# FNet mixing and a SwiGLU block on one core: the first chunk's preparation in another order, the split gate at another unit, the transforms one unit earlier

## The chip, the cores and the metric

The kernel runs on one core of one Trainium2 chip. The metric is the device time of one execution in microseconds (us). A core has five engines that run side by side, each through its own list of instructions in order: PE multiplies matrices (PEld is its loading of weights), DVE does elementwise work, ACT does elementwise work with functions (sine, SiLU, copies), POOL does elementwise work without access to PSUM and issues some transfers, and SP issues most transfers (DMA). They wait for each other by semaphores. Matmul results are written to PSUM, which has eight banks of 128 x 512 float32; all other tiles lie in SBUF.

## The reference

```python
def _attn_ref(x):                    # x: 8 x 3008 x 256
    X = np.fft.fft(x, axis=1)
    X = np.fft.fft(X, axis=2)
    return X.real.astype(np.float32)

def _moe_ref(x, w_gate, w_val, w_out):        # 24064 x 256, Dff = 1536
    g = x @ w_gate
    silu = g * (1.0 / (1.0 + np.exp(-g)))
    val = x @ w_val
    return (silu * val @ w_out).astype(np.float32)
```

The output of the first is the input of the second. The result is 24064 x 256 in float32.

## The kernel before, in words

**The mathematics.** The Fourier transform along the sequence (length M = 3008 per batch, 8 batches) is folded by symmetry: rows r and M - r, and the quarters of the sequence, are added and subtracted, so that a product with a quarter of the table (`Tab`, made on the chip from sines and cosines) is enough. The transform along the 256 features is not carried out on the data; it is multiplied into the weights. So there are two half inputs, an even one `Pt` and an odd one `Qt`, and two transformed weights, `Wp` (cosine) and `Wq` (sine); a row is Pt Wp + Qt Wq, and its mirror image in the sequence is Pt Wp - Qt Wq. `Wm` is -2 Wq (its row 0 zeroed by `m2`), so that adding Qt Wm to a finished accumulator turns a row's result into that of its mirror image. Each weight has a gate half (index 0) and a value half (index 1).

**The folds.** A batch's rows are treated as chunk A (128 rows of each quarter) and chunk C (60 more, and row 0 of the sequence). For batch 0 the rows are loaded to `XA` and `XC0`, and PE, DVE and ACT take part in the preparation: PE brings rows to their places by a product with a permutation (`place`, L417 to L425), DVE adds the mirrored rows (`sums`, L427 to L432), ACT writes the halves in bfloat16 (`halves`, `minus`, L434 to L439), and PE multiplies these unfolded halves with the table (`unfolded`, L448 to L464; eo = 0 makes Pt, eo = 1 makes Qt; ch = 0 is chunk A, ch = 1 chunk C). For the other batches POOL does the folding (`fold_steps`, L186 to L217) and PE the product (`transform`, L607 to L668). POOL also folds batch 0, for the second part of its frequencies (L552 to L567).

**The order of the preparation of batch 0** is written out by hand (L504 to L571 and L672 to L679), and each engine executes its instructions in just this order of the program: place and sums of A, halves of A, the second table, `d_tables`, unfolding of A for eo 0 and eo 1, weighting of the table (`weigh`), loads of the second weight third, POOL's steps on the table (L524 to L530), loads of the third; place, sums, halves of C; the transforms of the first third of the weights (`transform_w`, L467 to L483, for gate and value, each with CD and SDt); folds of A and of C on POOL, with the load of `Wo` between; loads of the next batch on SP; then unfolding of C, `transform` of batch 0's first part, which on DVE writes Pt and Qt, and `value_rows` (L485 to L502), products of one column that give the weights' share of row 0 in `w0`.

`transform_w` has two halves: two matmuls, and copies to SBUF that run when the returned function is called. The copies are one for `Wp` (k = 0, on DVE or ACT, L482), and for `Wq` (k = 1) one on ACT (L476) and then one multiply on POOL that makes `Wm` (L480; on ACT for the second third, L478). The first third's `Wm` is read from the first unit on.

**The main loop** (L1045 to L1081) runs over units (t, f): 24 tiles t of up to 512 columns, 12 blocks f of 128 of Dff. The tiles are 480, 512, 512 wide, the same again, 17 of 512, and a last one of 320. `part_a` multiplies gate g and value v with Pt and Qt; ACT forms SiLU(g) (`sg`) and DVE the product `hp` (L882, L898). In the next unit `part_b` adds the Wm product (L907), which gives the mirrored g (and v, in units that aren't split), and the mirrored product `hm` is formed by POOL (L912) or DVE (L916). Units that are `split` get the mirrored value without PE: DVE keeps the even part in `es` (L874) and takes 2 es - v (L885, L888). Tile 0 is all whole units. In `seeded` units (f in SEED = 1, 3, 10) ACT puts row 0's share into the accumulator (L809) and copies es (L872), which saves DVE its step L874. Between these products, PE does `OWork`: the product of the previous tile's hp and hm with `Wo` (L770), eight matmuls a unit, evicted by ACT (L730) and stored by SP (L736).

**The split gate.** In units with f in GATED and t >= 4, if split, the mirrored gate too comes from DVE: `gate_even` (L814) starts the gate product one unit early and DVE keeps its even part `eg` (L823), `gate_odd` (L827) adds the Qt product, and `mirrored` (L835) forms 2 eg - g. This saves PE one matmul of the tile's width, and costs DVE two steps. GATED is (2,): the gate's share of row 0 is an extra column of `w0`, made in `value_rows` of the weight third to which f belongs (thirds of four blocks).

**The transforms in the loop.** Batch b has two parts, (b, 0) and (b, 1). `slot` (L919) says at which unit the transform of a part is emitted: 4 units into the tile before the one that needs it; its second half (eo = 1) comes one unit later for part 0 and two units later for part 1. `seq` (L921 to L936) spreads POOL's folds ahead of these slots. Part (0, 1) is at unit 9 in both kernels.

`psG` and `psV` are lines of three PSUM banks each, used in turn; `psO` has two.

Of the kernel before, what the change touches and what calls it, by code (L numbers as in the profile page):

```python
# [31 lines left out]
def kernel(  # L32
# [8 lines left out]
    nc = tc.nc  # L41
# [61 lines left out]
    Tab = const.tile([P, 2, 2, 2, NTAB], BF16, name="Tab")  # L103
    halfpi = const.tile([P, 1], F32, name="halfpi")
    zero = const.tile([P, 1], F32, name="zero")
    GATED = (2,)
    w0 = const.tile([P, nF + len(GATED)], F32, name="w0")
    sel = const.tile([P, P], BF16, name="sel")
    CD = const.tile([P, 2, P], BF16, name="CD")
# [253 lines left out]
    def weigh(lo, hi):  # L363
        vts(Tab[:, 1, 1, :, lo:hi], Tab[:, 1, 1, :, lo:hi], scalar1=wC, scalar2=None, op0=Alu.mult)
# [73 lines left out]
    def minus(SB, S, a=0):  # L438
        nc.scalar.activation(SB[:, 2, a:a + 2], S[:, a:a + 2, :, P:D], AF.Copy, scale=-1.0)  # L439
# [27 lines left out]
    def transform_w(fc, gv, k, ps):  # L467
        dst, tab = ((Wp, CD), (Wq, SDt))[k]
        src = W0[gv] if fc == 0 else Wraw[gv][:, :, (fc - 1) * T:fc * T]
        fs = slice(fc * T, (fc + 1) * T)  # L470
        for no in range(2):
            nc.tensor.matmul(ps, tab[:, no, :], src[:, no, :], start=(no == 0), stop=(no == 1))

        def copies():
            if k:
                nc.scalar.copy(dst[:, gv, fs], ps)  # L476
                if fc == 1:
                    nc.scalar.activation(Wm[:, gv, fs], ps, AF.Copy, scale=m2)  # L478
                else:
                    pts(Wm[:, gv, fs], dst[:, gv, fs], scalar1=m2, scalar2=1.0, op0=Alu.mult, op1=Alu.mult)  # L480
            else:
                (nc.scalar.copy if gv and fc else nc.vector.tensor_copy)(dst[:, gv, fs], ps)  # L482
        return copies  # L483

    def value_rows(fcs):  # L485

        n = T // P
        ps = psO.tile([P, T], F32, name="o")
        for fc in fcs:
            src = W0[1] if fc == 0 else Wraw[1][:, :, (fc - 1) * T:fc * T]  # L490
            for f in range(n):
                for no in range(2):
                    nc.tensor.matmul(ps[:, fc * n + f:fc * n + f + 1], src[:, no, f * P:(f + 1) * P],
                                     SDt[:, no, 0:1], start=(no == 0), stop=(no == 1))
        nc.scalar.copy(w0[:, fcs[0] * n:(fcs[-1] + 1) * n], ps[:, fcs[0] * n:(fcs[-1] + 1) * n])
        for k, f in enumerate(GATED):
            if f // n in fcs:
                src = W0[0] if f < n else Wraw[0][:, :, (f // n - 1) * T:f // n * T]
                for no in range(2):
                    nc.tensor.matmul(ps[:, nF + k:nF + k + 1], src[:, no, f % n * P:(f % n + 1) * P],  # L500
                                     SDt[:, no, 0:1], start=(no == 0), stop=(no == 1))
                nc.scalar.copy(w0[:, nF + k:nF + k + 1], ps[:, nF + k:nF + k + 1])  # L502

    psA = place(XA, putA, 4, ((psG, "g"), (psV, "v")))  # L504
    sums(SA, XA, psA)
# [11 lines left out]
    d_tables()  # L517
    nc.vector.memset(SDt[:, :, 0:1], 1.0)
    unfolded(0, 0, SBa, True, False)
    unfolded(1, 0, SBa, True, False)  # L520
    weigh(0, NCE)

    load_w(1)
    nc.gpsimd.iota(kfO, pattern=[[4, G]], base=1, **iota)  # L524
# [4 lines left out]
    ptt(hd, SA[:, 0:2, :, 0:1], SA[:, 2:4, :, 0:1], op=Alu.add)  # L529
    heads(nc.gpsimd, hd[:, 0], hd[:, 1], CEa)  # L530
    load_w(2)
    psC = place(XC0, putC, 2, ((psO, "o"),))
    sums(SC, XC0, psC)
    halves(SBc, SC)
    minus(SBc, SC)
    wts = []
    for gv in range(2):
        for k, (pool, nm) in enumerate((((psV, "v"), (psG, "g")), ((psO, "o"), (psO, "o")))[gv]):
            wts.append(transform_w(0, gv, k, pool.tile([P, T], F32, name=nm)))
    heads(nc.vector, SC[:, 0, :, 0:1], SC[:, 1, :, 0:1], CEc)  # L540
    raO = SD.rearrange("p k a d -> p (k a d)")[:, 0:4 * G].rearrange("p (c q n) -> p c q n", c=2, q=2)

# [133 lines left out]
            row0(CE, slice(0, P), q, ch, q, acc[1][q])  # L676
    unfolded(1, 1, SBc, False, True)
    transform(0, 0, (1,), acc)
    value_rows((0,))  # L679

    tmp_ctx.close()
# [156 lines left out]
    def part_a(u):  # L838
        t, f = u
        n = width(t)  # L840
        w = n + (B if t == nT - 1 else 0)
        fs = slice(f * P, (f + 1) * P)
        if f == 0:
            hts[t] = (hp.tile([P, nF, T + B], BF16, name="hp"), hp.tile([P, nF, T], BF16, name="hm"))
        Pt, Qt = pq_tiles(t)

        def mm(ps, Wt, gv, src, start, stop):
            nc.tensor.matmul(ps[:, :w], Wt[:, gv, fs], src[:, :w], start=start, stop=stop,  # L848
                             skip_group_check=True)

        if gated(u):
            g, sg, _ = gates[u]
        else:
            g = psG.tile([P, T], F32, name="g")
            mm(g, Wp, 0, Pt, True, False)
            if u == (0, 0):
                v = psV.tile([P, T], F32, name="v")
                mm(v, Wp, 1, Pt, True, False)
            mm(g, Wq, 0, Qt, False, True)
        if split(u):  # L860
            mine = u in seeded
            e = seeded.pop(u) if mine else psV.tile()
            mm(e, Wp, 1, Pt, not mine, False)
            if not mine:
                psV.begun[id(e)] = w
            if not gated(u):
                sg = sgp.tile([P, T], F32, name="sg")
                nc.scalar.activation(sg[:, :w], g[:, :w], AF.Silu)  # L868
            stt = nc.vector.scalar_tensor_tensor
            es = next_es()  # L870
            if mine:
                nc.scalar.copy(es[:, :n], e[:, :n])  # L872
            else:
                stt(es[:, :n], bc[t][:, :n], w0[:, f:f + 1], e[:, :n], op0=Alu.mult, op1=Alu.add)  # L874

            def odd():
                if mine:
                    nc.tensor.matmul(e[:, :w], Wz[:, SEED.index(f), :], Qt[:, :w], start=False, stop=True,  # L878
                                     skip_group_check=True)
                else:  # L880
                    mm(e, Wq, 1, Qt, False, True)
                nc.vector.tensor_tensor(hts[t][0][:, f, :w], sg[:, :w], e[:, :w], op=Alu.mult)  # L882
# [12 lines left out]
        mm(v, Wq, 1, Qt, False, True)  # L895
        sg = sgp.tile([P, T], F32, name="sg")
        nc.scalar.activation(sg[:, :w], g[:, :w], AF.Silu)  # L897
        nc.vector.tensor_tensor(hts[t][0][:, f, :w], sg[:, :w], v[:, :w], op=Alu.mult)  # L898
        state[u] = (g, v)
# [221 lines left out]
```

## Time and profile before

| | |
|---|---|
| time, median of 3 runs | 625.33 us (625.13 to 625.45) |
| the profiled execution | 625.21 us |
| its span, first to last instruction | 623.3 us |
| busy: PE / DVE / POOL / ACT | 98% / 92% / 85% / 76% of the span |
| moved by DMA | 55.42 MB, mean 89 GB/s |
| unit (0,0) begins on PE | 23.66 us |

The profile gives busy time and share of each engine, and the trace lists every instruction with start and duration on the span's clock. In rows of a timeline, the first number is the start and the second the duration of a group of equal instructions that follow each other (x4 is four of them); in brackets stands how long the engine was idle before it, and what ended the wait. L and a number is the line of the kernel. Matmuls are pipelined: a row's duration holds the latency of the last, and a stream of them is read from start to start. In a table of windows, each row is a stretch from A to B with its length and then each engine's busy time in it. The rows that matter stand in the prediction.

### The profile page before, as it was taken

The page shows a single profiled execution, that of the slowest core. Times are in us where ns is not written, and L with a number is a line of the kernel's source. Part 1 is how long each engine was busy: PE and PEld are TensorE (multiplying, and loading weights), DVE is VectorE, ACT ScalarE, POOL GpSimd, SP SyncE. Part 2 cuts the span into 40 slices and gives each one's busy share as a digit, 9 for nine tenths or more (in the row PEclk, how much of TensorE's full clock was granted, in tenths as well). Part 3 has the DMA queues.
Part 4 walks back from the last instruction along what each step waited for, and adds up shares of the span by engine and source line. Part 5 has one row for each costly group of instructions (what it writes and reads, how often), then busy time and mean ns, then how long its engine had stood idle before and what let it go on. Part 6 is the DMA issues. An engine that isn't in the chain of part 4 may idle for free.

```text
span 623.3 us, 13287 instructions
## 1 busy us (share of the span) xinstructions
PE 610.8 (98%) x4124; PEld 396.4 (64%) x4190; DVE 575.3 (92%) x1053; ACT 470.8 (76%) x880; POOL 527.2 (85%) x543
## 2 busy tenths in 40 slices
PE   9999999999999999999999999999999999999997
PEld 6446666666666666666666666666666666666686
DVE  7889999999999999999999999999999999999991
ACT  7687868778777787787777877877787778778773
POOL 9997989899899989997997989998799856656661
PEclk9999999999999999999999999999999999999999
DMA  8682442244222253244245111134121111111112
GB/s 226 122 171 77 114 139 84 84 115 138 81 67 86 70 151 108 74 134 127 70 109 149 50 44 55 48 85 139 58 59 37 53 45 42 59 52 44 58 52 77
DMA packets 52981, 55.42 MB, mean 89 GB/s; under 512 B 7504, under 2 KB 44238, under 8 KB 52910
## 3 DMA queue, kind: packets, MB, share of 16 engines
q1 hardware_dynamic: 49726, 52.20, 29.2%
q0 software_dynamic: 3184, 2.36, 2.6%
q8 instruction: 33, 0.54, 0.4%
q14 instruction: 38, 0.31, 0.2%
HBM read 32.22 MB, written 24.67 MB: 91 GB/s over the span
## 4 chain that ended last, share of the span: by engine, by line
PE 87%; DVE 6%; ACT 3%; issue 2%; DMA 1%; SPq 0%; POOL 0%; DVEq 0%; ACTq 0%
PE o L770 37%; PE v L848 18%; PE g L848 15%; PE g L907 8%; PE v L620 2%; PE v L878 2%; DVE hp L882 2%; DVE VV L888 1%; DMA XA<-in_x_dram 1%; PE g L620 1%; ACT EV L730 1%; PE g L819 1%; ACT sg L868 1%; PE g L832 1%; DVE hm L916 1%
## 5 line engine op out<-in xcount | busy, mean ns | idle before, releaser
L912 POOL TENSOR_TENSOR hm<-sgv,VV 128x512 bf16<-128x512 f32 (+2 forms) x258 | 322.7, 1258 | 76.7 <-DVE VV L888 66.2
L911 ACT ACTIVATE sgv<-g 128x512 f32<-128x512 f32 (+2 forms) x258 | 153.7, 596 | 62.3 <-PE g L907 55.9
L882 DVE TENSOR_TENSOR hp<-sg,v 128x512 bf16<-128x512 f32 (+2 forms) x273 | 184.1, 675 | 7.6 <-PE v L848 6.2
L868 ACT ACTIVATE sg<-g 128x512 f32<-128x512 f32 (+2 forms) x253 | 151.5, 599 | 30.9 <-PE g L848 20.9
L770 PE MATMUL o<-Wo,hp 128*128 128x256 bf16 (+2 forms) x1140 | 169.6, 273 | 0.1
L770 PE MATMUL o<-Wo,hm 128*128 128x256 bf16 (+2 forms) x1140 | 169.7, 273 | 0.0
L770 PEld LDWEIGHTS <-hm 128*128 128x128 bf16 (+2 forms) x1140 | 112.0, 98 | 70.4 <-issue 2.5
L770 PEld LDWEIGHTS <-hp 128*128 128x128 bf16 (+2 forms) x1140 | 112.0, 98 | 67.8 <-issue 3.4
L888 DVE SCALAR_TENSOR_TENSOR VV<-SDf,v 128x512 f32<-128x512 f32 (+2 forms) x179 | 120.5, 673 | 0.0
L848 PE MATMUL v<-Pt,Wp 128*128 128x512 bf16 (+2 forms) x288 | 107.9, 375 | 5.2 <-DVE hm L916 0.8
L848 PE MATMUL g<-Pt,Wp 128*128 128x512 bf16 (+2 forms) x268 | 100.7, 376 | 0.1
L907 PE MATMUL g<-Qt,Wm 128*128 128x512 bf16 (+2 forms) x267 | 100.0, 375 | 0.7 <-ACT sg L897 0.7
L874 DVE SCALAR_TENSOR_TENSOR SDf<-bc,w,v 128x512 f32<-128x512 bf16 (+2 forms) x116 | 85.1, 734 | 0.2
L848 PE MATMUL v<-Qt,Wq 128*128 128x512 bf16 (+2 forms) x222 | 83.1, 374 | 0.0
L848 PEld LDWEIGHTS <-Wp 128*128 128x128 bf16 x556 | 54.2, 98 | 41.3 <-issue 7.1
L848 PE MATMUL g<-Qt,Wq 128*128 128x512 bf16 (+2 forms) x205 | 76.5, 373 | 0.0
L874 DVE SCALAR_TENSOR_TENSOR es<-bc,w,v 128x512 f32<-128x512 bf16 (+2 forms) x91 | 66.9, 735 | 0.1
L809 ACT ACTIVATE v<-bc,w 128x512 f32<-128x512 bf16 (+2 forms) x66 | 45.2, 685 | 24.1 <-DVE VV L888 23.7
L730 ACT COPY EV<-o 128x512 f32<-128x512 f32 x90 | 52.8, 586 | 4.8 <-PE o L770 4.8
L888 DVE SCALAR_TENSOR_TENSOR VV<-es,v 128x512 f32<-128x512 f32 (+2 forms) x79 | 53.2, 673 | 0.0
L848 PEld LDWEIGHTS <-Wq 128*128 128x128 bf16 x490 | 47.9, 98 | 8.0 <-issue 0.5
L872 ACT COPY SDf<-v 128x512 f32<-128x512 f32 (+2 forms) x66 | 39.1, 592 | 0.0
(189 smaller groups left out, 642.5 us busy)
## 6 DMA issues: line engine op xcount, KB each, us to landing
out_dram<-EV SPq DMA_DIRECT2D x96, 128.0 KB
XA<-in_x_dram SPq DMA_DIRECT2D x32, 256.0 KB
XA<-in_x_dram SPq DMA_DIRECT2D x112, 64.0 KB
XC<-in_x_dram SPq DMA_DIRECT2D x210, 16.0 KB
XC<-in_x_dram SPq DMA_DIRECT2D x56, 60.0 KB
bc<-row SPq DMA_DIRECT2D x20, 128.0 KB
out_dram<-EV SPq DMA_DIRECT2D x12, 120.0 KB
out_dram<-EV SPq DMA_DIRECT2D x10, 112.0 KB
```

Of the source, the lines that this page charges most:

```text
L730: nc.scalar.copy(ev[:, 0:len(pair), :], ps[:, 0:len(pair), :])
L770: nc.tensor.matmul(ps[:n, j, :], hts[minus][:, f, c:c + n], Wo[:, f, :], start=(f == 0), stop=(f == nF - 1))
L809: nc.scalar.activation(e[:, :w], bc[t][:, :w], AF.Copy, scale=w0[:, f:f + 1])
L848: nc.tensor.matmul(ps[:, :w], Wt[:, gv, fs], src[:, :w], start=start, stop=stop, skip_group_check=True)
L868: nc.scalar.activation(sg[:, :w], g[:, :w], AF.Silu)
L872: nc.scalar.copy(es[:, :n], e[:, :n])
L874: stt(es[:, :n], bc[t][:, :n], w0[:, f:f + 1], e[:, :n], op0=Alu.mult, op1=Alu.add)
L882: nc.vector.tensor_tensor(hts[t][0][:, f, :w], sg[:, :w], e[:, :w], op=Alu.mult)
L888: stt(vm[:, n - 1::-1], es[:, :n], 2.0, e[:, :n], op0=Alu.mult, op1=Alu.subtract)
L907: nc.tensor.matmul(ps[:, :w], Wm[:, gv, f * P:(f + 1) * P], Qt[:, :w], start=False, stop=True, skip_group_check=True)
L911: nc.scalar.activation(sg[:, w - 1::-1], g[:, :w], AF.Silu)
L912: nc.gpsimd.tensor_tensor(hts[t][1][:, f, :w], sg[:, :w], v[:, :w], op=Alu.mult)
```

## The change

It does three things, in one diff.

1. In the preparation of batch 0, `place` and `sums` of chunk C stand between the two unfoldings of A, and `halves` and `minus` of C behind the weighting of the table. The transforms of the value half of the first weight third move behind the unfolding and transform of C, to stand ahead of `value_rows`; the gate half stays where it was. The copy of a value half's `Wp` is always on ACT. In unit (0,0) the four products come in the order g, g, v, v instead of g, v, g, v.
2. The split gate is at f = 11 instead of 2. Its column of `w0` so comes from the last third of the weights; `value_rows` issues its products ahead of the first copy. In the last tile f = 11 is a whole unit, so there the gate is not split.
3. `slot` is 3 units into the tile instead of 4: transforms are emitted at units 3 and 4 (part 0) or 3 and 5 (part 1).

```diff
-    GATED = (2,)
+    GATED = (11,)
...
-                (nc.scalar.copy if gv and fc else nc.vector.tensor_copy)(dst[:, gv, fs], ps)
+                (nc.scalar.copy if gv else nc.vector.tensor_copy)(dst[:, gv, fs], ps)
...
+        more = [(k, f) for k, f in enumerate(GATED) if f // n in fcs]
+        for k, f in more:
+            src = W0[0] if f < n else Wraw[0][:, :, (f // n - 1) * T:f // n * T]
+            for no in range(2):
+                nc.tensor.matmul(ps[:, nF + k:nF + k + 1], src[:, no, f % n * P:(f % n + 1) * P],
+                                 SDt[:, no, 0:1], start=(no == 0), stop=(no == 1))
         nc.scalar.copy(w0[:, fcs[0] * n:(fcs[-1] + 1) * n], ps[:, fcs[0] * n:(fcs[-1] + 1) * n])
-        for k, f in enumerate(GATED):
...
+        for k, f in more:
+            nc.scalar.copy(w0[:, nF + k:nF + k + 1], ps[:, nF + k:nF + k + 1])
...
     unfolded(0, 0, SBa, True, False)
+    psC = place(XC0, putC, 2, ((psO, "o"),))
+    sums(SC, XC0, psC)
     unfolded(1, 0, SBa, True, False)
     weigh(0, NCE)
+    halves(SBc, SC)
+    minus(SBc, SC)
...
     load_w(2)
-    psC = place(XC0, putC, 2, ((psO, "o"),))
-    sums(SC, XC0, psC)
-    halves(SBc, SC)
-    minus(SBc, SC)
-    wts = []
-    for gv in range(2):
-        for k, (pool, nm) in enumerate((((psV, "v"), (psG, "g")), ((psO, "o"), (psO, "o")))[gv]):
-            wts.append(transform_w(0, gv, k, pool.tile([P, T], F32, name=nm)))
+    wts = [transform_w(0, 0, k, pool.tile()) for k, pool in enumerate((psV, psG))]
...
     transform(0, 0, (1,), acc)
+    for fn in [transform_w(0, 1, k, psO.tile([P, T], F32, name="o")) for k in range(2)]:
+        fn()
     value_rows((0,))
...
-            if u == (0, 0):
-                v = psV.tile([P, T], F32, name="v")
-                mm(v, Wp, 1, Pt, True, False)
...
-        if u != (0, 0):
-            v = psV.tile([P, T], F32, name="v")
-            mm(v, Wp, 1, Pt, True, False)
+        v = psV.tile([P, T], F32, name="v")
+        mm(v, Wp, 1, Pt, True, False)
...
-    slot = {(b, part): max(first_tile[(b, part)] - 1, 0) * nF + 4 for b, part in jobs}
+    slot = {(b, part): max(first_tile[(b, part)] - 1, 0) * nF + 3 for b, part in jobs}
```

More of the change, by code (lines that the diff above doesn't have):

```diff
@@ L494, in value_rows @@
                                      SDt[:, no, 0:1], start=(no == 0), stop=(no == 1))
-        nc.scalar.copy(w0[:, fcs[0] * n:(fcs[-1] + 1) * n], ps[:, fcs[0] * n:(fcs[-1] + 1) * n])
-        for k, f in enumerate(GATED):
[L497 to L502, printed above, removed]
+        more = [(k, f) for k, f in enumerate(GATED) if f // n in fcs]
[4 more added lines that the diff above has]
+                                 SDt[:, no, 0:1], start=(no == 0), stop=(no == 1))
+        nc.scalar.copy(w0[:, fcs[0] * n:(fcs[-1] + 1) * n], ps[:, fcs[0] * n:(fcs[-1] + 1) * n])
+        for k, f in more:
+            nc.scalar.copy(w0[:, nF + k:nF + k + 1], ps[:, nF + k:nF + k + 1])
     psA = place(XA, putA, 4, ((psG, "g"), (psV, "v")))
```

## The prediction

> **What bounds the kernel now.** I read the table of engines first, then busy times by stage, then each engine's timeline up to 40 us.
>
> ```profile
> PE 610.8 (98%) x4124; PEld 396.4 (64%) x4190; DVE 575.3 (92%) x1053; ACT 470.8 (76%) x880; POOL 527.2 (85%) x543
> ```
> ```profile
> 26.40:48.80 22.40, 20.43 (x109) 9.53 (x110) 17.86 (x33) 19.40 (x41) 20.72 (x33) 1.00 0.71 149
> 48.80:600.00 551.20, 545.95 (x3691) 355.21 (x3753) 525.50 (x931) 423.81 (x792) 475.99 (x451) 1.00 0.29 82
> ```
>
> The first row gives PE 98% of the span. The other two are stages: length, then busy time of PE, PEld, DVE, ACT and POOL. From 48.8 us on PE lacks 551.20 - 545.95 = 5.25 us in 551. It has almost nothing to gain there and no slack in which lost time could be made up. In tile 0 (26.4 to 48.8) it lacks 22.40 - 20.43 = 1.97 us. So this kernel is PE's instruction stream in order, and every microsecond for which PE stands still early on is added to the end. What matters is when PE can do each step of the prologue. PE's timeline (start, duration, line):
>
> ```profile
> 13.52 0.81 PE L463 MATMUL v<-Tab,SBa 128*128 128x377 bf16 x4
> ...
> 16.09 1.88 PE L422 MATMUL o<-XC,putC 128*128 128x512 f32 x4
> 17.81 0.38 PE L472 MATMUL v<-W,CD 128*128 128x512 bf16 x1
> ...
> 18.83 0.60 PE L472 MATMUL o<-W,CD 128*128 128x512 bf16 x2
> ...
> 19.70 0.89 PE L463 MATMUL v<-Tab,SBc 128*128 128x377 bf16 x4
> ...
> 23.02 0.34 PE L493 MATMUL o<-SDt,W 128*128 128x1 bf16 x8
> ...
> 23.66 0.36 PE L848 MATMUL g<-Pt,Wp 128*128 128x480 bf16 x1
> ...
> 26.20 0.37 PE L907 MATMUL g<-Qt,Wm 128*128 128x480 bf16 x1
> 26.41 0.37 PE L907 MATMUL v<-Qt,Wm 128*128 128x480 bf16 x1
> ```
>
> It is a nearly unbroken chain: the second unfolding of A begins at 13.52, chunk C is placed at 16.09, gate weights follow at 17.81, value weights at 18.83, the unfolding of C at 19.70, and unit (0,0) at 23.66. The row at 26.41 is the one on which the forecast hangs: the mirrored value product of unit (0,0), which reads Wm's value half. The multiply L480 on POOL makes Wm:
>
> ```profile
> 17.52 0.82 POOL L367 TENSOR_SCALAR Tab<-Tab 128x752 bf16<-128x752 bf16 x1
> ...
> 18.87 0.79 POOL L373 DMA_DIRECT2D EV<-in_moe_w_gate_dram  x1
> 19.66 0.73 POOL L373 DMA_DIRECT2D EV<-in_moe_w_val_dram  x1
> 20.99 1.36 POOL L480 TENSOR_SCALAR Wm<-Wq,m 128x512 bf16<-128x512 bf16 x2 [0.60 <-ACT Wq L476]
> 22.31 1.08 POOL L198 TENSOR_TENSOR EOf<-SA 128x512 f32<-128x512 f32 x1
> ...
> 37.61 1.36 POOL L480 TENSOR_SCALAR Wm<-Wq,m 128x512 bf16<-128x512 bf16 x2
> ```
>
> Both halves, gate and value, are multiplied at 20.99 (x2, 0.68 us each), and only then does POOL start on the folds of A and C, which keep it busy from 22.31 to 37.61.
>
> **Part 1: value weights behind chunk C (the expensive part).** The change emits the value half's transforms after the folds in the program. PE's and ACT's share of them comes at the right time, but their POOL step does not: the multiply for the value half now stands in POOL's stream behind the whole fold sequence, in front of the two multiplies that were at 37.61 (the list of POOL's instructions has L480 x1 ahead of the folds and x3 behind them, where it had x2 and x2). PE cannot go past the product that reads it, since its matmuls run in order; behind it wait the weight transforms of the second third, units (0,2) on, and with them ACT and DVE.
>
> When is the multiply done? POOL's start of the folds first. It hangs on Part 2, which follows, by which the gate multiply begins at 21.92 and ends at 22.60, and the folds start at 22.6 instead of 22.31. The sequence itself takes 37.61 - 22.31 = 15.30 us; nothing in it needs PE, and I leave its length as it is. So the value multiply starts at 37.9 and ends at 38.6, and PE's product that began at 26.41 begins at **38.6: 12.2 us later**. Bounds: 36.5 if POOL's start isn't delayed at all and its folds run 1 us faster while DVE stands still; 39.2 if they run as much slower. What the shift of the multiply saves POOL early (0.68 us) is in this sum.
>
> **Part 2: chunk C between the unfoldings of A.** PE reaches the placement of C at 13.52 instead of 16.09, and it needs C's rows, row 0 of the sequence among them:
>
> ```profile
> 9.18 0.59 SPq L282 DMA_DIRECT2D XC<-in_x_dram  x1
> ```
> ```profile
> 15.60 0.30 SPq L167 DMA_DIRECT2D XC<-in_x_dram  x1
> ```
> ```profile
> 15.85 0.71 DVE L364 TENSOR_SCALAR Tab<-Tab,wC 128x754 bf16<-128x754 bf16 x1 [1.60 <-issue]
> ```
> ```profile
> 18.01 0.82 DVE L432 TENSOR_TENSOR SC<-o,XC 128x510 f32<-128x510 f32 x3 [0.17 <-PE o L422]
> ```
>
> Row 0 is SP's twelfth transfer, issued at 9.18. SP's issues take eight completion counters in turn, so that each waits for the eighth before it; the twentieth, at 15.60, waits for row 0. Nothing ahead of it on the queues moves, so the rows are there by 15.60 as before and PE stands still from 13.52 to about 15.6: 2.1 us (bounds: 0 if they were there at 13.52, 2.6 if only at 16.09). I take 2.1, since the counter's row is nearest. From there by lengths of the rows above: placing 17.81 - 16.09 = 1.72, to 17.32; the second unfolding of A 16.09 - 13.52 = 2.57, to 19.89; gate weights about 0.87, as the value weights took (19.70 - 18.83), to 20.76; the products of C 23.02 - 19.70 = 3.32, to 24.08; value weights 0.87, to 24.95; value rows some 0.25; unit (0,0) at 25.2 instead of 23.66, 1.5 later. The wait between the value rows and the gate's column goes with the gated unit. PE is at the critical product at 26.41 + 1.5 = 27.9, and stands there until 38.6. So the 1.5 us are covered by the longer wait and cost nothing of their own, except through POOL: DVE has C's sums done 18.83 - 16.09 = 2.74 after the placement began, 15.6 + 2.74 = 18.34; the weighting of the table, now behind them, 0.71 more, 19.05; POOL's L367 waits for it (17.52 before); then 18.87 - 17.52 = 1.35 to the third pair of weight loads, and 20.39 - 18.87 = 1.52 for issuing them (0.79 + 0.73): 21.92, the number used in Part 1. ACT's copy that feeds the multiply ends earlier: gate transforms at 20.76, plus some 0.7. The value half's Wp copy moves from DVE to ACT, before the units begin; nothing in those 10 us waits for either.
>
> **Part 3: after the standstill.** ACT and DVE have run dry.
>
> ```profile
> 30.56 0.36 PE L907 MATMUL g<-Qt,Wm 128*128 128x480 bf16 x1 [0.71 <-ACT sg L897]
> 31.25 0.36 PE L907 MATMUL v<-Qt,Wm 128*128 128x480 bf16 x1 [0.32 <-DVE hp L898]
> ```
>
> The 0.71 us that PE waited at 30.56 for ACT's backlog mostly goes: 0.5 back (at most 1.97 us, all that PE lacks in that stage). Against it stands PE's own pace after a pause:
>
> ```profile
> 1.03 5.66 PE L308 MATMUL o<-sel 128*128 128x128 bf16 x60 [1.03 <-DVE sel L263]
> ```
> ```profile
> 4.00:5.00 1.00, 1.00 (x12) 1.00 (x11) 1.00 1.05 403
> 5.60:6.40 0.80, 0.80 (x17) 0.80 (x16) 1.00 1.12 264
> ```
>
> These are L308's sixty equal matmuls at the start of the run, whole and in two windows: 12 touch the microsecond from 4.0, but 17 the 0.8 us from 5.6. From start to start they are 0.107 us apart and later 0.056; 42 at the one and 18 at the other make the 5.5 us to the next matmul. So PE begins at half its pace and needs 42 x 0.107 = 4.5 us to reach the full one, while the clock column says 1.00 in both windows. No row of this run shows what a pause in mid-run does: nothing (0), or the same again (half of 4.5 = 2.2 us of work lost). I take the latter, because 10.7 us of idling is a start over again. Worked through: from 26.41 to the product at 30.56, less its wait and rounding, PE has 3.3 us of work; at half pace for 4.5 us and full pace behind that it needs 5.5, against 4.15 in the trace, and then the wait on DVE behind it, 0.32, is gone too: net **0.9 later**, where at full pace it is 0.5 earlier.
>
> The Trainium skill, "TensorE: Matmul & The Clock Gate", Part 1, has such a rule: PE's clock falls to half after one idle window of about 3.4 us and needs about as long of sustained work to come back. By it the pause costs an estimated 1.7 us of work instead of 2.2, and the time is some 0.5 us under mine; were there no such gate, 1.4 us under mine. The trace agrees in the start of the run; the granted-clock column doesn't show it.
>
> **Part 4: gate at unit 11, transforms one unit earlier.** The columns of the work are the same but in one place: in the last tile unit 11 isn't split, so its gate saves no product, and unit 2's returns, 320 columns, 0.14 us from start to start. Otherwise the steady stage has nothing to give (5.25 us at most) and can only lose where DVE comes late:
>
> ```profile
> 373.34 0.68 DVE L882 TENSOR_TENSOR hp<-sg,v 128x512 bf16<-128x512 f32 x1
> ```
> ```profile
> 374.97 0.60 PE L770 MATMUL o<-Wo,hp 128*128 128x256 bf16 x4
> ```
> ```profile
> L835 DVE SCALAR_TENSOR_TENSOR g<-eg,g 128x512 f32<-128x512 f32 x19 | 13.1, 691 | 0.0
> ```
>
> The first row is the last product (unit 11) of a tile, done at 374.02; PE reads it in the last matmul of its group of four at 374.97, at about 375.2: 1.2 us to spare, in a tile with transforms. The gate puts L835, 0.69 us, ahead of that product; the gate's other DVE step falls into unit 10, which has one of its own less because it is seeded. So 0.5 us are left and I count 0. Range: 5.25 gained at the very most, realistically 1; lost, see the rivals. The transforms keep their number and columns; their folds on POOL move with them by one unit: 0.
>
> **The sum.** 623.3 + 12.2 + 0.9 + 0.1 = 636.5 us of span. The profiled execution took 625.21, 1.9 more than its span: **638.4 us**, against 625.21 of its own, or 625.33, the median of three. About 0.2% (1.25 us) is what a measurement of this kernel can tell from no change.
>
> **Rivals.**
> - *PE comes back at full pace*: 1.4 less, 637.0. For it: the clock column never falls in the trace. Against: the slow first matmuls beside a clock of 1.00.
> - *The tile boundary tears as well*: DVE is already busy 525.5 of 551.2 us, and if its lag of 0.69 comes on top of 0.74 from the gate's other step, 1.43 exceeds the 1.2 to spare, by 0.2 to 0.4 in 19 tiles: 4 to 8 us, about 644. Against: 0.5 left by the working above.
> - *The multiply isn't late*: POOL would run it when its input is ready, about 26, whatever stands ahead of it. It decides at 27.9, when PE arrives. Then only the 1.5 us of Part 2 are left, of which 0.71 at 30.56 and 0.32 at 31.25, where ACT and DVE now lead, and some of tile 0's other 0.9 us come back: 625.2 + 1.5 + 0.1 - 1.0 to 1.97 = 624.8 to 625.8, not slower. Against: in each timeline POOL's rows come in the order of the program, and the folds, whose inputs are ready, stand ahead.
> - *POOL's folds run faster while DVE idles and tile 0 gives back all it can*: 36.5 and 1.97: about 634.
>
> **How the numbers follow.** Forecast 0.62 (636.5 to 640); full pace 0.15; boundary 0.10; faster folds 0.09; multiply not late 0.04. The range from 634.8 to 641.6 takes in the first two, part of the last-but-one's upper half and the unknown costs (38.6 at 37.5 to 39.2, the clock from -0.5 to +1.5, the steady stage from -1 to +2), and leaves out the full boundary case and the case of no delay. Faster by over 0.2%: 0.02, within: 0.02, slower: 0.96, all but the case of the multiply.
>
> **What will show it.** PE's waits: one of 10 to 11 us on POOL's Wm, L480, in front of the mirrored value product (right if it ends near 38.6), and one of about 2 us on C's transfers before its placement at 15.6. POOL: one L480 near 22, three from 37.9 on, the second of these waiting for ACT. After 38.6, matmuls of 480 columns 0.4 us apart instead of 0.2 for about 4 us. From tile 1 on tiles as long as before. It is wrong if PE has no long wait on POOL, if the wait ends before 37, or if waits on DVE appear at each change of tile.

## The result, and the profile after

| | before | after |
|---|---|---|
| median (lowest to highest), 4 runs each | 625.39 us (625.13 to 625.76) | 648.12 us (647.12 to 649.44) |
| ratio, 95% interval | | 1.0364 (1.0345 to 1.0382) |
| profiled execution, its span | 625.21, 623.3 us | 647.12, 645.3 us |

The change costs 22.7 us. The sign was right; the forecast, 638.4 us, is 9.7 us short and its range ends 6.5 us below the measured time. Of the lines named below, those of the changed kernel stand two to four lower than the same statements before (L907 is L903, L888 is L885, L874 is L871, L911 is L907, L916 is L912); L480, L770, L809, L835 and L848 are the same in both.

The table of engines, after, answers to the row of before with PE at 98%:

```profile
PE 622.3 (96%) x4191; PEld 397.0 (62%) x4191; DVE 575.8 (89%) x1050; ACT 471.6 (73%) x881; POOL 528.2 (82%) x543
```

PE has one load more (4191 for 4190) and a share of 96%, though the span is 22.0 us longer: by busy time PE seems to have done 11.5 us more of work. Most of it is not work, as will be seen.

**Where the 22 us lie.** The weight loads of PE are the best milestones: their counts, 4190 and 4191, differ by the one product more of the last tile, while the trace of before lacks some 60 records of matmuls (4124 for 4190 loads). From the first load of tile 0's output product to the first of tile 23's, before and then after (start, duration, line):

```profile
49.06 0.52 PEld L770 LDWEIGHTS <-hp 128*128 128x128 bf16 x4
...
611.47 0.78 PEld L770 LDWEIGHTS <-hp 128*128 128x128 bf16 x7
```
```profile
62.04 0.52 PEld L770 LDWEIGHTS <-hp 128*128 128x128 bf16 x4
...
633.48 0.78 PEld L770 LDWEIGHTS <-hp 128*128 128x128 bf16 x7
```

The same stretches as windows (length; busy time and count of PE, PEld, DVE, ACT, POOL; clock; DMA share; GB/s), before and after:

```profile
49.06:611.47 562.41, 557.16 (x3786) 364.45 (x3848) 534.91 (x951) 430.48 (x807) 482.04 (x458) 1.00 0.28 82
```
```profile
62.04:633.48 571.44, 566.56 (x3850) 364.30 (x3849) 536.28 (x949) 430.35 (x807) 478.91 (x455) 1.00 0.28 80
```

Ahead of tile 0's mark the changed kernel has lost 62.04 - 49.06 = 12.98 us. Between the marks it takes 571.44 instead of 562.41 us: 9.03 more, with one load more, the same clock, and 9.4 us more of "busy" PE. Behind them nothing: 633.48 - 611.47 = 22.01, and the spans differ by 22.0 (the profiled execution of the changed kernel is the fastest of its four, so this is 0.7 less than the medians give). So there are two losses, of which the prediction had one.

**The first loss**, as PE's waits over the whole run show it (us in total, times, longest):

```profile
PE v L903 <- POOL Wm L480: 10.8, 1, 10.8
PE v L848 <- ACT v L809: 2.4, 7, 0.4
PE o L422 <- issue: 1.6, 1, 1.6
```

The first row is the predicted wait for the value half's multiply, the third the predicted wait of chunk C's placement. PE's timeline, after:

```profile
15.27 1.95 PE L422 MATMUL o<-XC,putC 128*128 128x512 f32 x4 [1.62 <-issue]
...
25.20 0.36 PE L848 MATMUL g<-Pt,Wp 128*128 128x480 bf16 x1
...
38.82 0.58 PE L903 MATMUL v<-Qt,Wm 128*128 128x480 bf16 x1 [10.78 <-POOL Wm L480]
...
42.90 0.61 PE L903 MATMUL v<-Qt,Wm 128*128 128x480 bf16 x1
43.30 0.48 PE L848 MATMUL g<-Pt,Wp 128*128 128x480 bf16 x1
43.62 0.37 PE L848 MATMUL g<-Qt,Wq 128*128 128x480 bf16 x1
43.82 0.37 PE L848 MATMUL v<-Pt,Wp 128*128 128x480 bf16 x1
```

Placement at 15.27 (forecast 15.6), unit (0,0) at 25.20 (25.2), the critical product at 38.82 (38.6). Behind it equal matmuls are 0.40 us apart until 43.30, 4.5 us long, and then 0.20. On POOL's timeline the cause stands in the order of the program:

```profile
22.43 0.70 POOL L480 TENSOR_SCALAR Wm<-Wq,m 128x512 bf16<-128x512 bf16 x1
23.09 1.09 POOL L198 TENSOR_TENSOR EOf<-SA 128x512 f32<-128x512 f32 x1
...
38.07 0.69 POOL L480 TENSOR_SCALAR Wm<-Wq,m 128x512 bf16<-128x512 bf16 x1
```

The gate half's multiply, then 38.07 - 23.09 = 14.98 us of folds, then the value half's.

**The second loss** is spread over the tiles. The lag behind the kernel before, at the mark of each tile: 12.98 us at tile 0, 13.18 at tile 5, 19.03 at tile 14, 22.01 at tile 23. It grows by 0.65 us a tile from 5 to 14 (5.85 over nine tiles) and by 0.33 behind that. The list of waits shows only 2.4 us of it. The reason is how PE's rows are to be read: a matmul of 512 columns lasts 0.38 us in its row but follows its forerunner after 0.22, so that a gap of up to 0.16 hides behind the forerunner's tail and even a longer one counts as busy in part. Gaps must be read from start to start. The busy time misleads in one way more: before, 62 of the matmul records between the marks are missing (3786 for 3848 loads), and each leaves an apparent gap of 0.05 us, some 3 of the 9.4 us by which PE seems busier after. Around the change from tile 9 to tile 10, after, PE:

```profile
289.11 0.38 PE L848 MATMUL g<-Qt,Wq 128*128 128x512 bf16 x1
289.81 0.38 PE L848 MATMUL v<-Pt,Wp 128*128 128x512 bf16 x1 [0.32 <-ACT v L809]
...
291.54 0.38 PE L848 MATMUL g<-Qt,Wq 128*128 128x512 bf16 x1
291.76 0.38 PE L848 MATMUL v<-Pt,Wp 128*128 128x512 bf16 x1
...
293.57 0.38 PE L848 MATMUL g<-Qt,Wq 128*128 128x512 bf16 x1
294.06 0.38 PE L848 MATMUL v<-Pt,Wp 128*128 128x512 bf16 x1
```

These are units 1, 2 and 3 of tile 10. In unit 2 the value product follows after 0.22 us, in unit 1 after 0.70, in unit 3 after 0.49; only the first of these two has a wait noted. PE lost 0.48 and 0.27. Summed so over all tiles from 1 on, the distances beyond 0.22 come to 4.17 us ahead of unit 1 (in 12 tiles) and 4.91 ahead of unit 3 (in 19), where the kernel before has 0.03 and 0.30. That is 8.75 more, of 9.03; the rest are pieces of both signs (19 times 0.08 lost at unit 1's product with Wz, which is -0.5 Wm and stands in seeded units in place of Wq; about 1.1 us less ahead of the other units). In most tiles of before, the record of the g product ahead of unit 3 is missing; there the distance from the record in front of it is 0.43 us, two products without a gap.

What both are waiting for is the seed of that unit, L809, which ACT writes into the value bank before PE may add to it. ACT, after:

```profile
289.06 0.69 ACT L809 ACTIVATE v<-bc,w 128x512 f32<-128x512 bf16 x1 [0.68 <-DVE VV L885]
290.39 0.60 ACT L907 ACTIVATE sgv<-g 128x512 f32<-128x512 f32 x1 [0.63 <-DVE g L835]
...
292.79 0.64 ACT L865 ACTIVATE sg<-g 128x512 f32<-128x512 f32 x1
293.27 0.74 ACT L809 ACTIVATE v<-bc,w 128x512 f32<-128x512 bf16 x1
```

And DVE, after:

```profile
288.35 0.68 DVE L885 SCALAR_TENSOR_TENSOR VV<-SDf,v 128x512 f32<-128x512 f32 x1
288.95 0.74 DVE L871 SCALAR_TENSOR_TENSOR SDf<-bc,w,v 128x512 f32<-128x512 bf16 x1
289.61 0.69 DVE L835 SCALAR_TENSOR_TENSOR g<-eg,g 128x512 f32<-128x512 f32 x1
```

Unit 1's seed starts at 289.06 because the value bank it writes is free only when DVE's L885 is done (288.35 + 0.68). Then ACT stands idle again: next in its list is the mirrored SiLU of the gated unit 11, L907, which needs the gated unit's DVE step L835, and that stands on DVE behind L871, the first step of the next tile's unit 0. ACT starts it at 290.39, and from there runs without a break up to unit 3's seed, which ends at 293.27 + 0.74 = 294.01; PE's product begins at 294.06. The waits of ACT over the run have a row that the kernel before does not have at all:

```profile
ACT sgv L907 <- DVE g L835: 12.0, 19, 0.6
```

19 times 0.6 us: once in every tile with the gate at unit 11. For contrast the kernel before with its gate at unit 2, DVE and then ACT, in tile 10:

```profile
277.75 0.68 DVE L888 SCALAR_TENSOR_TENSOR VV<-SDf,v 128x512 f32<-128x512 f32 x1
278.35 0.69 DVE L835 SCALAR_TENSOR_TENSOR g<-eg,g 128x512 f32<-128x512 f32 x1
```
```profile
279.14 0.63 ACT L911 ACTIVATE sgv<-g 128x512 f32<-128x512 f32 x1
```

There unit 3 behind the gate is seeded, so DVE has no L874 for it and L835 comes directly; it is done at 279.04, and ACT's SiLU needs no wait.

### The profile page after: what moved, and what is told of

It is laid out like the page before. It is cut to its first block, busy times and chain, and to the rows that moved or that the text cites. A ratio compares the mean times of both kernels' runs of the same rounds, so it can differ in the third digit from the quotient of the medians.

```text
span 645.3 us, 13332 instructions
## 1 busy us (share of the span) xinstructions
PE 622.3 (96%) x4191; PEld 397.0 (62%) x4191; DVE 575.8 (89%) x1050; ACT 471.6 (73%) x881; POOL 528.2 (82%) x543
## 4 chain that ended last, share of the span: by engine, by line
PE 66%; DVE 11%; ACT 10%; issue 5%; POOL 4%; DMA 3%; SPq 0%; DVEq 0%; ACTq 0%; POOLq 0%
PE o L770 27%; PE v L848 13%; PE g L848 12%; PE g L903 6%; DVE hp L879 4%; ACT v L809 3%; PE v L618 3%; DVE VV L885 2%; ACT sg L865 2%; DMA XA<-in_x_dram 2%; ACT sgv L907 1%; ACT SDf L869 1%; DVE Qt L650 1%; PE v L875 1%; PE g L618 1%
## 5 line engine op out<-in xcount | busy, mean ns | idle before, releaser
L907 ACT ACTIVATE sgv<-g 128x512 f32<-128x512 f32 (+2 forms) x258 | 154.2, 598 | 87.3 <-PE g L903 70.2
L865 ACT ACTIVATE sg<-g 128x512 f32<-128x512 f32 (+2 forms) x254 | 153.1, 603 | 25.2 <-PE g L848 20.2
L770 PE MATMUL o<-Wo,hm 128*128 128x256 bf16 (+2 forms) x1140 | 169.7, 273 | 0.0
L770 PE MATMUL o<-Wo,hp 128*128 128x256 bf16 (+2 forms) x1140 | 169.6, 272 | 0.0
L770 PEld LDWEIGHTS <-hp 128*128 128x128 bf16 (+2 forms) x1140 | 111.7, 98 | 78.3 <-issue 15.0
L770 PEld LDWEIGHTS <-hm 128*128 128x128 bf16 (+2 forms) x1140 | 112.1, 99 | 67.5 <-issue 0.2
L885 DVE SCALAR_TENSOR_TENSOR VV<-SDf,v 128x512 f32<-128x512 f32 (+2 forms) x179 | 120.2, 672 | 0.0
L848 PE MATMUL v<-Pt,Wp 128*128 128x512 bf16 (+2 forms) x288 | 108.0, 375 | 4.9 <-ACT v L809 2.4
L848 PE MATMUL g<-Pt,Wp 128*128 128x512 bf16 (+2 forms) x269 | 101.3, 377 | 0.1
L848 PE MATMUL g<-Qt,Wq 128*128 128x512 bf16 (+2 forms) x269 | 100.9, 375 | 0.0
L903 PE MATMUL g<-Qt,Wm 128*128 128x512 bf16 (+2 forms) x269 | 100.9, 375 | 0.0
L871 DVE SCALAR_TENSOR_TENSOR SDf<-bc,w,v 128x512 f32<-128x512 bf16 (+2 forms) x116 | 85.0, 733 | 0.1
L848 PE MATMUL v<-Qt,Wq 128*128 128x512 bf16 (+2 forms) x222 | 83.3, 375 | 0.0
L848 PEld LDWEIGHTS <-Wp 128*128 128x128 bf16 x557 | 54.6, 98 | 41.9 <-issue 8.1
L871 DVE SCALAR_TENSOR_TENSOR es<-bc,w,v 128x512 f32<-128x512 bf16 (+2 forms) x91 | 66.9, 735 | 0.2
L809 ACT ACTIVATE v<-bc,w 128x512 f32<-128x512 bf16 (+2 forms) x66 | 46.1, 699 | 12.4 <-DVE VV L885 12.2
L848 PEld LDWEIGHTS <-Wq 128*128 128x128 bf16 x491 | 48.2, 98 | 8.4 <-issue 1.4
L885 DVE SCALAR_TENSOR_TENSOR VV<-es,v 128x512 f32<-128x512 f32 (+2 forms) x79 | 53.1, 672 | 0.0
L903 PEld LDWEIGHTS <-Wm 128*128 128x128 bf16 x284 | 27.9, 98 | 20.7 <-POOL Wm L480 11.2
```

The costliest lines, as they stand in the source:

```text
L770: nc.tensor.matmul(ps[:n, j, :], hts[minus][:, f, c:c + n], Wo[:, f, :], start=(f == 0), stop=(f == nF - 1))
L809: nc.scalar.activation(e[:, :w], bc[t][:, :w], AF.Copy, scale=w0[:, f:f + 1])
L903: nc.tensor.matmul(ps[:, :w], Wm[:, gv, f * P:(f + 1) * P], Qt[:, :w], start=False, stop=True, skip_group_check=True)
L907: nc.scalar.activation(sg[:, w - 1::-1], g[:, :w], AF.Silu)
```

## The experiments

My theory after the result: the loss is a sum of two parts that have nothing to do with each other, the late multiply (some 12.6 us) and the gate at unit 11 (some 9), the latter through ACT's and DVE's lists as above. Rivals: the slot moved to unit 3 causes the second part; the two parts are coupled, so that the late start tears the steady stage; the first part is the placement or PE's clock rather than POOL's order. Times are medians; "against" gives the difference from the kernel before on the same chip, which took 625.4 to 625.6 us there. Experiments made from the kernel before have its line numbers.

| run | what it is | us | against | ratio (95%) |
|---|---|---|---|---|
| e1_gate | before, gate at 11 alone | 635.01 | +9.6 | 1.0154 (1.0139 to 1.0169) |
| e2_slot | before, slot 3 alone | 627.74 | +2.3 | 1.0038 (1.0023 to 1.0053) |
| e3_prologue | the preparation alone | 638.01 | +12.6 | 1.0203 (1.0186 to 1.022) |
| e4_after_act | after, value multiply on ACT | 636.13 | +10.7 | 1.0177 (1.0162 to 1.0192) |
| e5_prologue_act | e3 with the same edit | 626.27 | +0.9 | 1.0013 (1.0003 to 1.0022) |
| e6_prologue_warm | e3, PE kept busy in the pause | 636.91 | +11.5 | 1.0186 (1.0171 to 1.0201) |
| e7_gate_early | e1, L835 ahead of the next unit | 628.83 | +3.4 | 1.0054 (1.0039 to 1.0069) |
| e8_nogate | before, no gate | 627.05 | +1.6 | 1.0026 (1.0016 to 1.0036) |
| e9_gate_early_light | e7, DVE relieved in tiles 4 to 13 | 625.76 | +0.2 | 1.0009 (1.0 to 1.0018) |
| e10_after_repaired | after, both repairs | 629.94 | +4.4 | 1.0077 (1.0062 to 1.0093) |
| e11_two_gates | before, a second gate late | 627.82 | +2.3 | 1.0037 (1.0024 to 1.0049) |
| e12_light | before, DVE relieved alone | 626.24 | +0.7 | 1.0012 (1.0003 to 1.0021) |

### The three parts one by one: e1_gate, e2_slot, e3_prologue

```diff
# e1_gate, from before
-    GATED = (2,)
+    GATED = (11,)
# e2_slot, from before
-    slot = {... * nF + 4 for b, part in jobs}
+    slot = {... * nF + 3 for b, part in jobs}
# e3_prologue, from after: both of these set back
```

> The kernel before with the split gate at unit 11 and nothing else. Theory A (the gate at the tile boundary makes the loss of the steady stage: DVE's two extra steps come just ahead of the seeds of units 1 and 3, which wait in ACT's and DVE's queues): 8 to 10 us slower than before, 633.5 to 635.5, PE's gaps ahead of the value product of units 1 and 3 in nearly every tile from 4 on. Theory B (the transforms one unit earlier make it): within 1 us of before.

> The kernel before with the transforms one unit earlier and nothing else. Theory A: within 1 us of before. Theory B: 8 to 10 us slower. If both are needed together, this and the gate alone are each well under 9 us.

> The changed order of the preparation alone, gate at unit 2 and transforms as before. The prediction's Parts 1 to 3 by themselves: 13 us slower than before, 638.3, with one wait of PE on POOL of about 10.8 us. If the late start of tile 0 also disturbs the steady stage, 640 or more.

The gate alone costs 9.6 us without any late start, so it needs no coupling, and the preparation alone 12.6: at 638.0 it lands on the forecast of the whole change. In e1's trace the two gaps are those of the changed kernel: 4.3 us ahead of unit 1 in 12 tiles, 4.9 ahead of unit 3 in 19. The slot alone costs 2.3 us, which I had not expected. In e2 PE's waits between 49 and 620 us have one row that neither the kernel before nor after has:

```profile
PE g L848 <- ACT sgv L911: 1.7, 6, 0.3
```

The sum of the three, 12.6 + 9.6 + 2.3 = 24.5, is more than the 22.7 of the whole, and with the gate at 11 the slot costs far less (next section). So most of its cost comes only together with the gate at unit 2; that this is because the two are neighbours in the tile is likely, but not shown.

### POOL's order: e4_after_act, e5_prologue_act

```diff
-                if fc == 1:
+                if fc == 1 or (fc, gv) == (0, 1):
```

This lets ACT make the value half's Wm of the first third, as it already does for the second third, and leaves POOL's folds where they are.

> The changed kernel, with the value half's Wm made by ACT straight from the transform's result, so that it no longer stands behind POOL's folds. Theory (the multiply's place in POOL's list is what costs the 13 us): the long wait goes, with it the slow clock; what is left is 1.5 us of the placement's wait less what tile 0 gives back, 0 to 1.5, and the 9 us of the steady stage: 634.5 to 636. Rival (the order of the preparation costs by itself, through the earlier placement of chunk C): 640 or more.

> The changed order of the preparation alone, with the value half's Wm made by ACT. Theory: POOL's place for the multiply is 11 to 12.5 us of the 12.6 that this order costs; without it PE has only the placement's wait of 1.6 to 2 us, of which tile 0 gives some back: 625.4 to 627, no wait of PE on POOL. Rival (the earlier placement and the moved transforms cost by themselves): 630 or more.

It takes 12.0 us from the changed kernel (648.12 to 636.13, 0.1 above the range expected) and 11.7 from e3 (638.01 to 626.27). So 11.7 to 12.0 of the preparation's 12.6 us are POOL's order and what follows from it, and 0.9 is all the rest of the rearrangement. PE's wait ahead of the placement is still there in e5, and PE still waits for ACT in tile 0:

```profile
15.56 1.96 PE L422 MATMUL o<-XC,putC 128*128 128x512 f32 x4 [2.21 <-issue]
...
32.38 0.36 PE L903 MATMUL g<-Qt,Wm 128*128 128x480 bf16 x1 [0.90 <-ACT sg L893]
```

e4 and e5 differ by the gate and the slot together: 636.13 - 626.27 = 9.9 us, 0.3 more than the gate alone, which is within what two medians can tell. Step by step from the changed kernel back to the one before, that is 12.0 (POOL), 9.9 (gate and slot) and 0.9 (rest of the preparation); that these make up the whole follows from how they are formed. What speaks for two separate causes is that each has nearly the same size with and without the other: 12.0 and 11.7 for POOL's order, 10.1 (648.12 - 638.01) and 9.9 for gate and slot.

### PE's pace after the pause: e6_prologue_warm

Ahead of the waiting product, in unit (0,0) alone:

```diff
+            if u == (0, 0) and gv == 1:
+                warm = psO.tile([P, T], F32, name="o")
+                for j in range(48):
+                    nc.tensor.matmul(warm[:, :w], sel, Pt[:, :w], start=True, stop=True)
```

It adds 48 matmuls whose result nobody reads.

> The changed order of the preparation alone, with 48 additional matmuls of 480 columns (their result is not used) ahead of the product that waits for POOL, so that PE is busy for 9.7 of the 10.8 us. If PE's slow pace behind the pause is a matter of its idling, the matmuls behind it are 0.20 us apart at once and the time is 1.2 to 1.7 less than without them, 636.3 to 636.8. If the pace has another reason: the same 638.0.

PE's timeline of e3, without them, and then of e6:

```profile
39.48 0.58 PE L903 MATMUL v<-Qt,Wm 128*128 128x480 bf16 x1 [10.77 <-POOL Wm L480]
...
41.97 0.59 PE L848 MATMUL g<-Qt,Wq 128*128 128x480 bf16 x1
42.37 0.40 PE L848 MATMUL v<-Pt,Wp 128*128 128x480 bf16 x1
42.60 0.37 PE L848 MATMUL v<-Qt,Wq 128*128 128x480 bf16 x1
```
```profile
28.07 9.88 PE L906 MATMUL o<-Pt,sel 128*128 128x480 bf16 x48
38.95 0.38 PE L907 MATMUL v<-Qt,Wm 128*128 128x480 bf16 x1 [1.00 <-POOL Wm L480]
...
40.03 0.37 PE L848 MATMUL g<-Pt,Wp 128*128 128x480 bf16 x1
40.23 0.37 PE L848 MATMUL g<-Qt,Wq 128*128 128x480 bf16 x1
```

With PE kept busy, the matmuls behind the pause are 0.20 us apart at once; without, 0.40 until 42.4, and then 0.23 and 0.20. The time falls by 1.1 us by medians (638.01 to 636.91), a little less than the 1.2 to 1.7 expected, and 1.6 by spans (636.2 to 634.6). Of these 1.6, 0.5 are not PE's pace: in e6 the waiting product begins 0.53 us earlier, since POOL's steps from L367 on (18.72 us instead of 19.20) run about that much earlier. That leaves 1.1 for the pace, under the 1.4 between the two cases of the prediction. The runs of the two kernels overlap (637.25 to 638.86, 636.58 to 638.21), so the amount is rough; the distances are not.

### The gate's path: e7_gate_early, e8_nogate, e9_gate_early_light

```diff
# e7_gate_early, from e1: L835 is issued before part_a of the next unit
+        if prev in mirrored:
+            mirrored.pop(prev)()
         coming = part_a(u)
         if i not in job_at and i + 1 < len(units):
             seed(units[i + 1])
-        if prev in mirrored:
-            mirrored.pop(prev)()
# e8_nogate, from before
-    GATED = (2,)
+    GATED = ()
# e9_gate_early_light, from e7: unit 8 on POOL from tile 4 on, not from 14
-    LIGHT = 14
+    LIGHT = 4
```

> The gate alone at unit 11, with DVE's step 2 eg - g (L835) one step earlier, ahead of the even part of the next unit instead of behind it. If PE's loss comes through ACT, whose mirrored SiLU of the gated unit waits 0.6 us for this step and delays the seed of unit 3 behind it: 2 to 5 us less than the gate's 635.0, and the gaps ahead of unit 3 shrink. If it comes from DVE's total work ahead of the boundary, whichever step is first: 634.5 to 635.5, and the gaps stay.

> The kernel before without any split gate: 20 units pay one matmul more, 19 of 0.216 us and one of 0.14, 4.2 us of PE, and DVE has two steps less in each. If PE's work alone sets the steady stage: 629.6. If the gate at unit 2 also costs waits: less than that. At unit 11 the gate (635.0) is then worse than no gate by 5 us: its waits cost more than twice what its matmul saves.

> The gate alone at unit 11 with L835 first, and unit 8's mirrored product on POOL instead of DVE from tile 4 on (before: from tile 14). If the gaps that are left ahead of unit 1 in tiles 5 to 13 (4.3 us) come from DVE's being late by its load ahead of the boundary, they go: 624 to 625.5, unless POOL becomes late in its place. If they come from the seeds' place in ACT's queue: 628.8 as without it.

e7 gives back 6.2 of the 9.6 us, more than the 2 to 5 expected. At the same place between two tiles (14 and 15) DVE, ACT and PE of e7:

```profile
399.59 0.69 DVE L835 SCALAR_TENSOR_TENSOR g<-eg,g 128x512 f32<-128x512 f32 x1
400.18 0.74 DVE L874 SCALAR_TENSOR_TENSOR SDf<-bc,w,v 128x512 f32<-128x512 bf16 x1
```
```profile
400.37 0.60 ACT L911 ACTIVATE sgv<-g 128x512 f32<-128x512 f32 x1
```
```profile
404.13 0.38 PE L848 MATMUL g<-Qt,Wq 128*128 128x512 bf16 x1
404.35 0.38 PE L848 MATMUL v<-Pt,Wp 128*128 128x512 bf16 x1
```

L835 now comes first, ACT's SiLU no longer waits, and unit 3's value product follows after 0.22 us: over the run the gaps ahead of unit 3 fall from 4.91 us in the changed kernel to none. Those ahead of unit 1 stay (12 tiles, 4.27 us). 4.0 us of them lie in tiles 5 to 14, each right behind a tile from 4 to 13, in which DVE also makes the mirrored product of unit 8; e9 moves that to POOL from tile 4 on, and of the 4.27 us 0.26 are left. The time falls by a further 3.1 us, to 0.3 above the range expected. POOL now comes late once, in tile 10, ahead of a transform:

```profile
PE g L620 <- POOL CEa L209: 1.4, 1, 1.4
```

In this profiled execution that tile is 3.4 us longer than before, and PE's granted clock falls to 0.92 in the 4 us around the wait. But this execution took 627.77 us, 2.0 above the median, so how much the wait takes from a typical execution isn't shown.

e8 gives the measure for all of it: without any gate PE has 4.3 us more of matmuls (one product of 0.22 us in each of 19 tiles, and 0.14 in the last) and the kernel takes only 1.6 us more: part of the rest it gets back in waits, since PE's gaps ahead of units 5 and 10 fall from 2.7 us to 0.6. The gate at unit 2 is worth 1.6 us, and at unit 11, with its steps in this order, it is 8 us worse than none (635.01 against 627.05).

### Repairing and recombining: e10_after_repaired, e11_two_gates, e12_light

```diff
# e10_after_repaired: after with e4's and e7's edits
# e11_two_gates, from before, with e7's edit
-    GATED = (2,)
+    GATED = (2, 11)
-        return u[0] >= 4 and u[1] in GATED and split(u)
+        return u[0] >= (4 if u[1] == 2 else LIGHT) and u[1] in GATED and split(u)
# e12_light, from before
-    LIGHT = 14
+    LIGHT = 4
```

> The changed kernel with both repairs: the value half's Wm made by ACT, and L835 ahead of the next unit's even part. Theory (two independent causes, the multiply's place in POOL's list and the gate's step in front of ACT): 648.1 - 12.0 - 6.2 = 629.9. If the two overlap or one hides another: 632 or more.

> The kernel before with a second split gate at unit 11 in tiles 14 to 22 only, where unit 8 no longer burdens DVE, and L835 first. Nine matmuls of 0.216 us less. If DVE has the room that the theory says (no waits at those boundaries): 1.9 us faster than before, 623.5. If it has not: 625 to 628.

> The kernel before with unit 8's mirrored product on POOL from tile 4 on and nothing else: what that does by itself, to compare with the gate at 11 with it. If DVE's load costs PE nothing at the gate's old place: within 0.5 us of before. If the waits ahead of unit 5 in seven tiles (2.1 us) are DVE's load too: 1 to 2 us faster.

e10 comes out at 629.94: the two repairs together give back what they gave singly. The gaps ahead of unit 1 (4.3 us) are left in it, as in e7. The other two missed. A second gate in the late tiles, which I expected to gain, costs 2.25 us: 0.67 us is gone at tile 0's mark, and from tile 15 to 22 each tile loses 0.1 to 0.3 us. PE's waits have a row for each. The late tiles pay ahead of a seeded unit, unit 3, again: there the distances from start to start are 0.40 us too long in each of tiles 15 to 22, 3.3 us in all with the last tile, for the 1.9 of matmuls saved. The loss in tile 0 is a longer wait for ACT's copy of the value rows:

```profile
PE v L848 <- ACT v L809: 1.9, 8, 0.2
PE o L500 <- ACT w L495: 1.1, 2, 0.8
```

So there is no room for a second gate there either; which of ACT and DVE lacks it was not tried. e12 shows that the relief of DVE gains nothing in the kernel before: POOL is late once, as in e9 (PE waits 1.1 us, and tile 10 is 1.6 us longer). No version beat the kernel before.

## Why the prediction was wrong, step by step

- **What bounds the kernel**: right: with one weight load more on PE, the 12.98 and the 9.03 us by which it came later are the whole of the span's 22.0. But I read PE's gaps off busy time. That hides the small ones, and some 3 of the 5.25 us that PE seemed to lack are no gaps at all, but missing records (3691 matmuls for 3753 loads in that row).
- **Part 1, the multiply on POOL**: right. The product begins at 38.82, forecast 38.6. That it came so near is in part luck: the folds began at 23.09 instead of the forecast 22.6, and took 14.98 us instead of 15.30. Tile 0's mark is 12.98 us late, where 12.2 + 0.9 = 13.1 was worked out. e4 and e5 show the cause.
- **Part 2, placement of chunk C**: right. PE waits 1.62 us, and 2.21 in e5, for 2.1; the placement begins at 15.27, and SP's twentieth issue, by which I dated the landing of row 0, is at 15.29; unit (0,0) begins at 25.20. Uncovered, in e5, the whole rearrangement costs 0.9 us, below the 1.5 of PE's delay.
- **Part 3, half pace after the pause**: right in its mechanism: 4.5 us at 0.40 apart instead of 0.20, and e6 takes it away. The length was luck. The 4.5 us came from one start of a run; over the fourteen traces the half pace of the first matmuls lasts from 2.8 to 5.8 us, and in e3, behind the same pause, 2.9. The cost was a little smaller too: the product came 12.41 us late and the mark 12.98, so 0.6 us were lost behind it, for 0.9 (the working's own terms, 5.5 - 4.15 - 0.32, give 1.0). The rival of full pace falls. Its support, a clock column that never falls, was weak: behind this pause the column does fall (below).
- **Part 4, gate at unit 11**: this is the step that failed, at "0.5 us are left and I count 0". It asked of the delay on DVE only when PE reads unit 11's product hp. The list of waits has no row of PE waiting for that, and the distances from start to start have no gap there. What came late first was something else on the same engines: ACT's list is in order, the gated unit's SiLU waits in it for L835, and the seeds behind it were late for PE; and DVE's lag freed the value bank of unit 1's seed late. The first is paid in each of 19 tiles (e7 takes it away), the second in tiles 5 to 14 above all, while DVE also makes unit 8's mirrored product (e9 takes it away). Measured: 9.0 us between the marks, 9.6 alone. The prediction had DVE's two steps as 1.43 us against 1.2 of slack, and never asked who waits behind the waiting instruction on ACT.
- **Slot at 3**: taken at nothing, and with the gate at 11 nothing that two medians resolve (0.3). With the gate at 2 it costs 2.3.
- **The rivals**: "the tile boundary tears as well" had the place right and the amount nearly (4 to 8 us foreseen, 9.0 measured, about 644 foreseen, 648.1 measured) but by another path. It had 0.10, because I set slack of one reader against it; DVE busy for 525.5 of 551.2 us, as the prediction itself has it, should have given it more. "The multiply isn't late" and "faster folds" fall with POOL's rows.

## What to carry to other kernels

When a step is moved on an engine that executes in order, list everything that stands behind it on that engine, and everything behind each instruction that waits for it on the next engine; the first late consumer need not be the one that reads the moved result. A small multiply that feeds the bottleneck belongs ahead of a long sequence that nobody needs yet, or on another engine: that alone was 12 of 22.7 us here. Read gaps on a pipelined engine from start to start, and over many tiles; 0.27 us that no list of waits shows was 4.9 us in all.

## What the hardware showed that was not expected

The granted clock in windows of the changed kernel and of e6, the third number from the right. The second row lies wholly within the pause:

```profile
28.00:40.00 12.00, 1.22 (x4) 0.43 (x4) 1.73 (x3) 1.16 (x3) 10.47 (x22) 0.72 0.71 119
34.00:38.00 4.00, 0.00 (x0) 0.00 (x0) 0.00 (x0) 0.00 (x0) 3.81 (x11) 0.50 1.27 183
40.00:45.00 5.00, 5.00 (x17) 2.04 (x16) 1.54 (x4) 4.41 (x8) 0.00 (x0) 0.65 0.52 137
```
```profile
28.00:40.00 12.00, 11.00 (x55) 5.10 (x53) 1.94 (x3) 1.55 (x4) 10.61 (x22) 1.00 0.72 120
```

In a pause of 10.8 us in mid-run the column falls to 0.50, which makes 0.72 and 0.65 of the two longer windows, and it stays at 1.00 where PE was kept busy. In the slow first matmuls of the run it had said 1.00, so for the start it cannot be used and behind a pause it can. The half pace lasted 4.5 us in the changed kernel (38.82 to 43.30) and 2.9 in e3 (39.48 to 42.37), behind pauses of the same length. The Trainium skill, "TensorE: Matmul & The Clock Gate", Part 1, says that an idle window of about 3.4 us halves the clock and that sustained work of about as long restores it, in windows that run freely. The traces agree with the halving, and with the return in order of size only.
